# Choosing the PSUM bank of each product by three estimated clocks instead of a queue, in a fused adaLN, multi-query attention and gated-FFN kernel

## The chip, the cores and the metric

The kernel runs on one core of one Trainium2 chip. The metric is the device time of one execution in microseconds (us); a time given for a kernel is the median of several runs. The profile is that of one profiled execution. Engines are named as in its pages: PE is TensorE (PEld its weight loads), DVE is VectorE, ACT is ScalarE, POOL is GpSimd, SP is the queue that issues most DMAs. L601 is line 601 of the kernel before; in the kernel after, the lines up to the new functions' end and behind them lie up to eleven further on (L601 becomes L611, L511 becomes L521, L847 and L849 become L858 and L860).

## The reference

One transformer block on x of 2048 x 512, in float32, with a conditioning vector c of 512:

```python
mod = (silu(c) @ w_mod).reshape(1, 6, 1, 512)        # sa, ca, ga, sb, cb, gb
h = layernorm(x) * (1 + ca) + sa
q, k, v = h @ wq, h @ wk, h @ wv                     # 32 query heads of 16; one key and one value head
o = softmax(q @ k.T * 16 ** -0.5) @ v
x = x + ga * (o @ wo)
h = layernorm(x) * (1 + cb) + sb
x = x + gb * (((h @ w_gate) * (h @ w_up)) @ w_down)  # inner width 1792
```

## The kernel before

**The work and its stages.** Sequence rows are cut in eight sub-blocks of 256 (`sb`) and the 32 heads in four chunks, which gives 32 attention units `u`. For a unit TensorE makes, per key tile of 128, the scores `sc` (L657, L659) that ScalarE turns into exponentials `P` (L661), and from these the sums `pv` (L670: four fp32 products, eight records in the profile). The softmax needs the row maxima: for the next unit TensorE makes products `mx` (L601) that VectorE reduces to one column (`mpart`, L605). For unit 0, in the start, the maxima of later keys are made in another way: a `diff` product (a bank named `sc`, two matmuls at L601) is clipped by ScalarE (`rel`, L608), and a `both` product (a bank named `mx`) is added to it and reduced by VectorE (L610).

Everything else is "side work" in groups (class `Group`, L491): the query projection, the output projection `wo`, gate and up products (24 matmuls of 128 x 256 where a group runs whole), and down products (42 of 128 x 512). A group accumulates in one bank named `side` (all at L511), and is then emptied: a gate/up group by `g` on ScalarE (L847) and `gf` on VectorE (L849), a `wo` or down group by one residual add on VectorE (L750, L865). Between the attention's matmuls the side work fills in as half-array products; there are styles of a turn (L58 to L60), without side work, with few and with many. After the last unit's last `pv` comes the tail: all groups still left run whole, one behind the other: the last gate/up and down groups of sub-block 6, the last `wo` (L735), the last layer norm with its transposes to `mx` banks (L805, emptied by two `hf` on ScalarE each, L813), and all 14 gate/up and 2 down groups of sub-block 7 (`cover`, `run`, L1327 to L1355).

**The order.** It is written out while the program is built: the code calls the products in the order in which each engine gets them, and no scheduler reorders them. The hardware's part is only the semaphores: the first matmul into a bank waits until the bank's last reader is done.

**The banks.** PSUM has eight banks of 128 x 512 floats, and `pool` (L77) is a queue of their names. `ps_hold` (L80) takes the bank at the queue's head, `ps_give` (L87) puts it at the end; `ps_mx` (L91) does both at once, so for `mx` and `sc` the queue turns with each product. `side` groups and `pv` hold their bank until they are emptied (L519, L677), one or two groups and one `pv` at a time. So a bank comes round again some five to seven allocations later, whoever read it.

**The staging slots.** In the start, weights are loaded into slots of 512 floats in `kwb` (`hfs`, L225; `SLOTS`, L35; `stage`, L931), where GpSimd squares them (L944, L946). The sums of squares `ssqs` (L226) lie in the same tile; the first one covers slots 4 to 7.5, so with slots 6 and 7 in `SLOTS` it shares their place. `kng` (L227), which only the `diff` products read, lies in the first half of slot 12.

Of the kernel before, what the change touches and what calls it, by code (L numbers as in the profile page):

```python
# [13 lines left out]
F32 = mybir.dt.float32  # L14
# [8 lines left out]
BT = S // NB  # L23
# [8 lines left out]
SQ_GAP = 2.6  # L32
LAG = 2
ROW_LAG = 4
SLOTS = (0, 1, 2, 3, 6, 7)  # L35
SUM_GAP = 4.0
SUM_LAG = 3
SPLIT_GAP = 2.5
# [1 line left out]
LATE_Q = 3  # L40
NORM_AT = (5, 12, 15, 19)
NBANK = 8
QPRE = 24
Q_LAG = 8
TR_WAIT = 11
# [18 lines left out]
def adaln_mqa_glu_kernel(ctx: ExitStack, tc: tile.TileContext, x_in, wq_in, wk_in, wv_in, wo_in,  # L64
# [9 lines left out]
    psum = ctx.enter_context(tc.tile_pool(name="psum", bufs=1, space=bass.MemoryType.PSUM))  # L74
    ctx.enter_context(tc.manual_schedule())

    pool = deque((f"bank{i}", 1) for i in range(NBANK))  # L77
    held = {}

    def ps_hold(name="side", shape=(128, 512)):  # L80

        tag, bufs = pool.popleft()
        t = psum.tile(list(shape), F32, name=name, tag=tag, bufs=bufs)
        held[id(t)] = (t, tag, bufs)
        return t

    def ps_give(t):  # L87
        _, tag, bufs = held.pop(id(t))
        pool.append((tag, bufs))

    def ps_mx(name="mx", shape=(128, 512)):  # L91
        t = ps_hold(name, shape)
        ps_give(t)
        return t

    def ps_sc():
        return ps_mx("sc")

    def ps_misc(shape=(128, 512)):
        return ps_mx("misc", shape)  # L100
# [45 lines left out]
    for i in range(3):  # L146
        t = consts.tile([128, 2, 2, ST], F16, name=f"sst{i}")
# [15 lines left out]
    nc.gpsimd.memset(selk, 0.0)  # L163
    nc.gpsimd.memset(selq, 0.0)
    pwarm = ps_hold("misc")

    def keep_warm(n):
# [17 lines left out]
    sil = consts.tile([128, KC], F32, name="sil")  # L185
    csb = consts.tile([128, KC], F32, name="csb")
    pc = ps_mx()
    nc.tensor.transpose(pc[:, 0:KC], c4, ident[0:KC, 0:KC])
    nc.scalar.activation(csb, pc[:, 0:KC], AF.Copy)
# [34 lines left out]
    kwb = big.tile([128, 2 * FT * D], F16, name="kwb", tag="wd")  # L224
    hfs = kwb[:, 0:2 * NHF * BT].bitcast(F32).rearrange("p (n t) -> p n t", n=NHF)  # L225
    ssqs = [kwb[:, 2 * n * BT:2 * n * BT + 2 * F].bitcast(F32) for n in (KC, 2 * KC)]  # L226
    kng = kwb[:, 2 * NHF * BT:2 * NHF * BT + BT]  # L227

    def hf(b, k):
# [33 lines left out]
    def ln_tr(b, ks=range(KC)):  # L263
        for k in ks:
            p = ps_sc()
            for t in range(4):
                nc.tensor.transpose(p[:, t * 128:(t + 1) * 128],
                                    xts[2 * b + t // 2][t % 2][:, k * 128:(k + 1) * 128], ident)
            bias, scale = (hsb[:, k, 0:1], hsb[:, k, 1:2]) if b else (modT[0][:, k, 0:1], modT[0][:, k, 32:33])
            nc.scalar.activation(hf(b, k), p, AF.Identity, bias=bias, scale=scale)  # L270
# [3 lines left out]
    def partial(key, ws, b):  # L274
        p = ps_hold("part")
        w = BT // len(ws)
        for j in range(KC):
            for c, wc in enumerate(ws):
                nc.tensor.matmul(p[32 * j:32 * j + 32, c * w:(c + 1) * w], wc[:, j], hf(b, j)[:, 0:w],
                                 start=True, stop=True)  # L280
        parts[key] = work.tile([128, BT], F32, name="part", tag="ev", bufs=3)
        nc.scalar.activation(parts[key], p, AF.Copy)
        ps_give(p)
# [11 lines left out]
    def q_evac(u, p):  # L295
        split_rows(sst[u][:, :, p, :], pks[u, p], qsc, sck[:, 3:4], 0.0)
        ps_give(pks[u, p])
# [122 lines left out]
    def wq_sum():  # L420
        p = ps_sc()
        nc.tensor.matmul(p[:, 0:4], ones, wst["acc"], start=True, stop=True)
        t = work.tile([128, 2], F32, name="wqt", bufs=1)
        nc.vector.tensor_reduce(t[:, 0:1], p[:, 0:4], axis=AX.X, op=OP.add)
        nc.gpsimd.tensor_tensor(t[:, 1:2], t[:, 0:1], phalf[:, 0:1], op=OP.pow)
        nc.gpsimd.tensor_scalar(inv[:, 1:2], t[:, 1:2], 1.001 * 2.0 ** -15, 2.0 ** -45, op0=OP.mult, op1=OP.max)
# [132 lines left out]
    def load_q(u):  # L559
        sb, ch = divmod(u, NC)  # L560
        d = qd[sb // 2, ch].rearrange("(h e) l n -> e h l n", e=16)
        s = sst[u % 3].rearrange("p c q n -> p (c q) n")
        n0 = (sb % 2) * ST
        for a in range(2):
            for r, hl in ((0, 0), (1, 0), (2, 1)):
                nc.sync.dma_start(s[64 * a + 16 * r:64 * a + 16 * r + 16, :, :], d[:, a::2, hl, n0:n0 + ST])
# [26 lines left out]
    def max_mm(u, a, op):  # L593
        kind, p, t, kc = op
        s = sst[u % 3]
        m = ps_sc() if kind == "diff" else ps_mx()
        keys = [kst[:, kc * 512:(kc + 1) * 512]]
        if kind == "diff":
            keys = [kng, kst[:, (kc + 1) * 512:(kc + 2) * 512]]
        for i, w in enumerate(keys):  # L600
            nc.tensor.matmul(m, s[64 * a:64 * a + 48, t // 2, p, t % 2 * 128:(t % 2 + 1) * 128], w[64 * a:64 * a + 48, :],  # L601
                             start=(i == 0), stop=(i == len(keys) - 1))
        part = mparts[u][:, a, 4 * (t // 2) + 2 * p + t % 2, kc:kc + 1]
        if kind == "one":
            nc.vector.tensor_reduce(part, m, axis=AX.X, op=OP.max)  # L605
        elif kind == "diff":
            r = rel[a] = work.tile([128, 512], F32, name="rel", tag="x1", bufs=6)
            relus.append(lambda: nc.scalar.activation(r, m, AF.Relu))  # L608
        else:
            nc.vector.tensor_tensor_reduce(out=rel[a], in0=m, in1=rel[a], scale=1.0, scalar=LOW, op0=OP.add,  # L610
                                           op1=OP.max, accum_out=part)  # L611
# [53 lines left out]
    def pv(u, kt):  # L665
        if kt == 0:
            pvb[u] = ps_hold("pv")
        for j in range(4):
            p, a = divmod(j, 2)
            nc.tensor.matmul(pvb[u][32 * j:32 * j + 32, :], vst[:, kt, :], ptl[u, kt, p, a],  # L670
                             start=(kt == 0), stop=(kt == KT - 1))
# [221 lines left out]
    def late_weights():  # L893
# [35 lines left out]
        taken = [0]  # L929

        def stage(n):  # L931
            if "d" in W:
                t = work.tile([128, D], F32, name="wsl", tag="xl", bufs=3)
            else:
                t = hfs[:, SLOTS[taken[0] % len(SLOTS)], :]
                taken[0] += 1
            nc.sync.dma_start(t[:, :sl[n][3]], sl[n][2])
            st[n] = t
# [24 lines left out]
        def norms(order):  # L963
            ns = [n for m in order for n in range(len(sl)) if sl[n][0] == m]
            out = []
            waiting = deque()
            for j in range(len(ns) + LAG):
                q = j - LAG

                def f(j=j, q=q):  # L970
                    if j < len(ns):
                        stage(ns[j])
                    if q >= 0:
                        square(ns[q])
                out.append((SQ_GAP, nothing, f))
                if waiting and j >= waiting[0][0]:
                    out.append((0,) + sums(*waiting.popleft()[1:]))
                if q >= 0 and (q == len(ns) - 1 or sl[ns[q]][0] != sl[ns[q + 1]][0]):
                    waiting.extend((j + SUM_LAG, sl[ns[q]][0], n) for n in range(4))
            out.append((SUM_GAP, nothing, nothing))  # L980
            return out + [(2,) + sums(*w[1:]) for w in waiting]
# [146 lines left out]
    def max_half(a):  # L1128
# [10 lines left out]
        u, i, last, ops = flat[n]  # L1139
        if 0 < u < NU - 1 and i == QPRE:  # L1140
            load_q(u + 1)
# [76 lines left out]
    def attend(u, kt):  # L1218
# [10 lines left out]
        def end_turn(kt):  # L1229
            for g in ended:  # L1230
                g.finish()
            ended.clear()
            for f in ends:
                f()
            ends.clear()
            v = u * KT + kt - 1
            if v >= 0:
                pv(*divmod(v, KT))
                if v % KT == KT - 1:
                    ends.append(lambda: pv_out(u - 1))  # L1240
            if not late_max() and turns and all(q.ended() for q in qs):
                _, f, post = turns.popleft()
                f()
                posts.append(post)
            hooks(u, 2 * kt + 1)
# [66 lines left out]
    u = NU - 1  # L1312

    pv(u, KT - 1)
    pv_out(u)
    sync["before"] = sync["exp"]
# [60 lines left out]
```

## Time and profile before

| | |
|---|---|
| median of 3 runs | 1665.09 us (1664.6 to 1665.9) |
| span of the profiled execution, first to last instruction | 1663.8 us |
| median less that span | 1.3 us |
| PE busy | 1643.3 us (99%) |
| DVE busy | 1402.3 us (84%) |
| ACT busy | 1234.8 us (74%) |
| POOL busy | 523.5 us (31%) |
| granted TensorE clock, mean | 0.998 |

The profiled execution has no time of its own beside the span. A row of a group gives line, engine, operation, tile written and read, and count; behind it the busy time, the mean of one in ns, the idle time of the engine just before, and what ended that. A row of the windows gives a stretch (from:to, us) and each engine's busy time in it, with the granted clock behind. A row in order of time gives start, duration and what; in square brackets stands the idle time before it and what released it. Matmuls overlap each other, so a busy PE may still issue late. The span falls in four parts: the start to about 80 us, attention with little side work to about 320 us, attention with side work to about 1552 us, and the tail.

### The profile page before, as it was taken

Reading aid. Unit: us, or ns where it says so; the run is one execution under the profiler, and the core shown is the slowest. Engines: PE = TensorE matmul, PEld = TensorE weight load, DVE = VectorE, ACT = ScalarE, POOL = GpSimd, SP = SyncE. Lnnn points to the kernel's source line nnn. Section 1 sums busy time; section 2 is a strip of 40 time slices with the busy share of each in tenths; the row PEclk is TensorE's granted clock in tenths of the full one; section 3 lists DMA queues with packets and bytes.
Section 4 is the critical chain, followed back from the end, with each engine's and each line's share of the span. In section 5 each row is a group of like instructions: output and inputs, shape, how many; then the busy total and the mean of one; then the engine's idle time right before and its main releaser. Section 6 shows DMA issues by size and latency. Waiting matters only on the chain.

```text
span 1663.8 us, 39821 instructions
## 1 busy us (share of the span) xinstructions
PE 1643.3 (99%) x15677; PEld 747.1 (45%) x15677; DVE 1402.3 (84%) x2434; ACT 1234.8 (74%) x2389; POOL 523.5 (31%) x833
## 2 busy tenths in 40 slices
PE   8899999999999999999999999999999999999999
PEld 4333333355533554335543355434545345454776
DVE  7999999998998999899998999999998999980211
ACT  5688888888777877777877787777878777877300
POOL 4857537864841111301112011300113001210322
PEclk9999999999999999999999999999999999999999
DMA  6313313342210001000000000000000000000100
GB/s 237 108 59 100 95 43 120 96 129 80 77 51 24 18 12 32 19 32 20 20 26 23 25 13 24 26 25 26 20 29 15 26 22 20 26 14 21 33 13 14
DMA packets 66024, 75.39 MB, mean 45 GB/s; under 512 B 17702, under 2 KB 46634, under 8 KB 65836
## 3 DMA queue, kind: packets, MB, share of 16 engines
q1 hardware_dynamic: 63724, 72.26, 13.7%
q8 instruction: 123, 2.02, 0.5%
q10 hardware_dynamic: 2112, 0.59, 0.1%
q14 instruction: 65, 0.53, 0.1%
HBM read 55.51 MB, written 17.04 MB: 44 GB/s over the span
## 4 chain that ended last, share of the span: by engine, by line
PE 93%; ACT 2%; DVE 2%; DMA 1%; issue 1%; POOL 0%; SPq 0%; ACTq 0%; DVEq 0%
PE side L511 41%; PE pv L670 30%; PE mx L601 8%; PE sc L659 8%; PE sc L657 3%; ACT P L661 2%; DVE mpart L605 1%; DMA xbig<-in_A_x_dram 1%; PE mx L805 1%; PE mxt L629 0%; ACT hf L813 0%; PE sc L601 0%; DVE bs L248 0%; DMA kwb<-in_B_w_down_dram 0%; DMA wkv<-in_A_wv_dram 0%
## 5 line engine op out<-in xcount | busy, mean ns | idle before, releaser
L605 DVE TENSOR_REDUCE mpart<-mx 128x1 f32<-128x512 f32 x2016 | 1274.1, 684 | 104.0 <-PE mx L601 95.7
L661 ACT ACTIVATE P<-sc 128x512 f32<-128x512 f32 x2048 | 1094.8, 598 | 274.2 <-PE sc L659 226.9
L601 PE MATMUL mx<-kst,sst 48*128 48x512 f16 x2032 | 631.5, 377 | 3.8 <-ACT P L661 1.7
L659 PE MATMUL sc<-sst,kst 50*128 50x512 f16 x1792 | 597.5, 379 | 0.6 <-ACT P L661 0.3
L670 PE MATMUL pv<-P,vst 128*32 128x512 f32 x4096 | 545.3, 605 | 0.7
L511 PE MATMUL side<-h2T,wg 64*128 64x256 f16 (+1 forms) x2396 | 540.8, 271 | 0.1
L511 PE MATMUL side<-h2T,wu 64*128 64x256 f16 (+1 forms) x2396 | 538.7, 270 | 0.0
L511 PEld LDWEIGHTS <-wg 64*128 64x128 f16 (+1 forms) x2396 | 226.0, 94 | 230.5 <-ACT P L661 194.0
L511 PE MATMUL side<-wd,glu 64*128 64x512 f16 (+1 forms) x1172 | 272.8, 378 | 0.2 <-ACT P L661 0.2
L850 POOL TENSOR_SCALAR glu<-gf 128x256 f16<-128x256 f32 x112 | 45.8, 409 | 671.3 <-DVE gf L849 583.9
L511 PEld LDWEIGHTS <-wu 64*128 64x128 f16 (+1 forms) x2396 | 226.4, 94 | 43.0 <-issue 7.8
L601 PEld LDWEIGHTS <-sst 48*128 48x128 f16 x2064 | 189.9, 94 | 34.2 <-issue 17.4
L659 PEld LDWEIGHTS <-kst 50*128 50x128 f16 x1792 | 162.9, 94 | 63.0 <-issue 50.3
L511 PEld LDWEIGHTS <-glu 64*128 64x128 f16 (+1 forms) x1172 | 98.5, 94 | 192.4 <-ACT P L661 85.9
L670 PEld LDWEIGHTS pv<-P,vst 128*32 128x32 f32 x4096 | 80.7, 108 | 160.9 <-issue 150.1
L849 DVE TENSOR_TENSOR gf<-side,g 128x256 f32<-128x256 f32 x112 | 46.7, 418 | 79.8 <-ACT g L847 77.7
L657 PE MATMUL sc<-sst,kst 50*128 50x256 f16 x512 | 96.9, 268 | 0.1
L511 PE MATMUL side<-h,wq 64*128 64x512 f16 (+1 forms) x372 | 95.0, 376 | 0.4 <-ACT P L661 0.4
L847 ACT ACTIVATE g<-side 128x256 f32<-128x256 f32 x112 | 42.3, 379 | 65.6 <-PE side L511 65.3
L511 PE MATMUL side<-wo,och 64*128 64x512 f16 (+1 forms) x360 | 86.3, 377 | 0.0
L851 POOL TENSOR_TENSOR glu<-gf,glu 128x256 f16<-128x256 f32 x112 | 75.3, 673 | 9.3
L706 POOL TENSOR_TENSOR oc<-oc,rr 128x256 f32<-128x256 f32 x31 | 22.7, 731 | 146.6 <-DMA rr<-ri 100.4
(233 smaller groups left out, 865.4 us busy)
## 6 DMA issues: line engine op xcount, KB each, us to landing
pd<-ev SPq DMA_DIRECT2D x32, 256.0 KB
kwb<-in_B_w_gate_dram SPq DMA_DIRECT2D x32, 224.0 KB
kwb<-in_B_w_up_dram SPq DMA_DIRECT2D x32, 224.0 KB
sst<-qd SPq DMA_DIRECT2D x180, 32.0 KB
qd<-q SPq DMA_DIRECT2D x16, 256.0 KB
oc<-pd SPq DMA_DIRECT2D x64, 64.0 KB
rr<-ri SPq DMA_DIRECT2D x64, 64.0 KB
x<-in_A_x_dram SPq DMA_DIRECT2D x14, 256.0 KB
```

What stands on the lines that cost most here:

```text
L511: return nc.tensor.matmul(self.p[:, c * w:(c + 1) * w], left[rows], right[rows], start=start and c == 0, stop=stop and c == len(terms) - 1)
L601: nc.tensor.matmul(m, s[64 * a:64 * a + 48, t // 2, p, t % 2 * 128:(t % 2 + 1) * 128], w[64 * a:64 * a + 48, :], start=(i == 0), stop=(i = ...
L605: nc.vector.tensor_reduce(part, m, axis=AX.X, op=OP.max)
L657: nc.tensor.matmul(t[:, c * ST:(c + 1) * ST], keys, s[64 * a:64 * a + 50, c, p, :], start=True, stop=True)
L659: nc.tensor.matmul(t.rearrange("k (c n) -> k c n", c=2), keys, s[64 * a:64 * a + 50, :, p, :], start=True, stop=True)
L661: ex = nc.scalar.activation(ptl[u, kt, p, a], t, AF.Exp)
L670: nc.tensor.matmul(pvb[u][32 * j:32 * j + 32, :], vst[:, kt, :], ptl[u, kt, p, a], start=(kt == 0), stop=(kt == KT - 1))
L706: eng.tensor_tensor(o, o, st["r"], op=OP.mult)
L847: nc.scalar.activation(g, p[:, 0:ST], AF.Copy, scale=2.0 ** -45)
L849: nc.vector.tensor_tensor(gf, p[:, ST:2 * ST], g, op=OP.mult)
L850: nc.gpsimd.tensor_scalar(glu()[:, 0, f, :], gf, 1.0, 0.0, op0=OP.mult, op1=OP.add)
L851: nc.gpsimd.tensor_tensor(glu()[:, 1, f, :], gf, glu()[:, 0, f, :], op=OP.subtract)
```

## The change

Each bank now carries a time at which its reader should be done. Three clocks `est` (for PE, ACT and DVE) are kept while the program is built, in the units of `EST`: each `ps_mx` product moves PE's clock by 0.22 and its reader's to the later of that clock and PE's plus 0.45, plus 0.49 (ACT) or 0.6 (DVE); each `pv` call moves PE's by 1.15. A product takes the bank with the least time (`min(banks)`: of equal times the lowest bank number), and PE's clock moves up to that time. A bank given back without an engine's name (by groups, `pv`, `part`, `pk` and the like) is marked with the largest of the three clocks, and no clock moves. Beside it two staging slots change from 6 and 7 to 12 and 13.

```diff
-SLOTS = (0, 1, 2, 3, 6, 7)
+SLOTS = (0, 1, 2, 3, 12, 13)
+EST = {"pe": 0.22, "lag": 0.45, "act": 0.49, "dve": 0.6, "pv": 1.15}
...
-    pool = deque((f"bank{i}", 1) for i in range(NBANK))
+    banks = [[0.0, i] for i in range(NBANK)]
+    est = {"pe": 0.0, "act": 0.0, "dve": 0.0}
     held = {}
 
     def ps_hold(name="side", shape=(128, 512)):
 
-        tag, bufs = pool.popleft()
-        t = psum.tile(list(shape), F32, name=name, tag=tag, bufs=bufs)
-        held[id(t)] = (t, tag, bufs)
+        b = min(banks)
+        banks.remove(b)
+        est["pe"] = max(est["pe"], b[0])
+        t = psum.tile(list(shape), F32, name=name, tag=f"bank{b[1]}", bufs=1)
+        held[id(t)] = (t, b[1])
         return t
 
-    def ps_give(t):
-        _, tag, bufs = held.pop(id(t))
-        pool.append((tag, bufs))
+    def ps_give(t, engine=None):
+        _, n = held.pop(id(t))
+        if engine is None:
+            free = max(est.values())
+        else:
+            est["pe"] += EST["pe"]
+            free = est[engine] = max(est[engine], est["pe"] + EST["lag"]) + EST[engine]
+        banks.append([free, n])
 
-    def ps_mx(name="mx", shape=(128, 512)):
+    def ps_mx(name="mx", shape=(128, 512), engine="dve"):
         t = ps_hold(name, shape)
-        ps_give(t)
+        ps_give(t, engine)
         return t
 
     def ps_sc():
-        return ps_mx("sc")
+        return ps_mx("sc", engine="act")
...
+    stg = kwb.bitcast(F32).rearrange("p (n t) -> p n t", t=BT)
...
     def pv(u, kt):
         if kt == 0:
             pvb[u] = ps_hold("pv")
+        est["pe"] += EST["pv"]
...
-                t = hfs[:, SLOTS[taken[0] % len(SLOTS)], :]
+                t = stg[:, SLOTS[taken[0] % len(SLOTS)], :]
```

The instructions of each engine keep their order; what differs is the bank of a tile and so the semaphore that its first matmul waits for. Two places on PE show it. In the rows, `sc_776` and the like are tiles with their numbers (equal in both kernels), and in brackets stand the engines whose semaphore is waited for (`Activation_49` ACT, `DVE_49` DVE, `PE_49` PE itself).

In the start, in the steps of `diff` (`sc`) and `both` (`mx`) products of unit 0, PE has before:

```order
L601 MATMUL sc_776<-kwb_181,sst0_128 128x512
L601 LDWEIGHTS sst0_128
L601 MATMUL sc_776<-kst_132,sst0_128 128x512
L601 LDWEIGHTS sst0_128
L601 MATMUL mx_786<-kst_132,sst0_128 128x512
```

and eight rows further on:

```order
L601 MATMUL mx_793<-kst_132,sst0_128 128x512 [waits DVE_49]
L601 LDWEIGHTS sst0_128
L601 MATMUL sc_796<-kwb_181,sst0_128 128x512 [waits DVE_49]
L601 LDWEIGHTS sst0_128
L601 MATMUL sc_796<-kst_132,sst0_128 128x512
```

The same places after:

```order
L611 MATMUL sc_776<-kwb_181,sst0_128 128x512 [waits Activation_49]
L611 LDWEIGHTS sst0_128
L611 MATMUL sc_776<-kst_132,sst0_128 128x512
L611 LDWEIGHTS sst0_128
L611 MATMUL mx_786<-kst_132,sst0_128 128x512
```

```order
L611 MATMUL mx_793<-kst_132,sst0_128 128x512
L611 LDWEIGHTS sst0_128
L611 MATMUL sc_796<-kwb_181,sst0_128 128x512 [waits Activation_49]
L611 LDWEIGHTS sst0_128
L611 MATMUL sc_796<-kst_132,sst0_128 128x512
```

A `diff` product now waits for ACT, where it waited for nothing or for DVE: `sc_776` has the bank of `sc_769`, `sc_796` that of `sc_776`, and so on; the `both` product `mx_793` waits for nothing any more.

In the tail, where the gate/up group that began before the last `wo` ends (`side_26291`) and the next one begins (`side_26394`), PE has before:

```order
L511 LDWEIGHTS wu_4056
L511 MATMUL side_26291<-h2T_4878,wu_4056 128x256
L511 LDWEIGHTS wg_4055
L511 MATMUL side_26394<-h2T_4878,wg_4055 128x256
L511 LDWEIGHTS wu_4056
```

and after:

```order
L521 LDWEIGHTS wu_4056
L521 MATMUL side_26291<-h2T_4878,wu_4056 128x256
L521 LDWEIGHTS wg_4055
L521 MATMUL side_26394<-h2T_4878,wg_4055 128x256 [waits DVE_49]
L521 LDWEIGHTS wu_4056
```

The first matmul of `side_26394` waited for nothing, since its bank had long been read; now it has the bank of `side_26291` and waits for DVE's read of that. The same difference stands in the gate/up groups of the last sub-block, before:

```order
L511 MATMUL side_26690<-h2T_4878,wu_4056 128x256
L511 LDWEIGHTS wg_4055 [waits PE_49]
L511 MATMUL side_26721<-h2T_4878,wg_4055 128x256 [waits Activation_49]
L511 LDWEIGHTS wu_4056
L511 MATMUL side_26721<-h2T_4878,wu_4056 128x256
```

and after:

```order
L521 MATMUL side_26690<-h2T_4878,wu_4056 128x256
L521 LDWEIGHTS wg_4055
L521 MATMUL side_26721<-h2T_4878,wg_4055 128x256 [waits DVE_49]
L521 LDWEIGHTS wu_4056
L521 MATMUL side_26721<-h2T_4878,wu_4056 128x256
```

Before, `side_26721` had the bank of the second transpose tile, seven allocations back, which ACT reads; after, that of `side_26690`, the group directly before it.

## Prediction

> **What bounds the kernel now.** I read the page's busy shares first, then the chain that ended last, then the windows of two stretches, and then the instructions in order of time at the places where a bank is waited for.
>
> ```profile
> span 1663.8 us, 39821 instructions
> PE 1643.3 (99%) x15677; PEld 747.1 (45%) x15677; DVE 1402.3 (84%) x2434; ACT 1234.8 (74%) x2389; POOL 523.5 (31%) x833
> PE 93%; ACT 2%; DVE 2%; DMA 1%; issue 1%; POOL 0%; SPq 0%; ACTq 0%; DVEq 0%
> ...
> core 0: us, PE busy (x) PEld busy (x) DVE busy (x) ACT busy (x) POOL busy (x), PEclk, DMA share, GB/s
> 320.00:1500.00 1180.00, 1176.83 (x11971) 539.52 (x11965) 1079.19 (x1820) 933.51 (x1806) 282.79 (x465) 1.00 0.11 32
> 1552.00:1660.00 108.00, 107.84 (x796) 77.58 (x793) 21.53 (x44) 13.62 (x32) 31.51 (x66) 1.00 0.06 21
> ```
>
> TensorE bounds it: 93% of the chain. But a busy PE hides small waits, since a matmul of 0.38 us is issued every 0.22 us. So for the middle stretch I count turns (one turn is one `pv` step of 8 recorded matmuls), and set them against a turn in which nothing waits:
>
> ```profile
> 320.00:1500.00 1180.00, 429.94 (x3232) 63.44 (x3224) 17.11 (x25) 1.00 0.11 32
> ...
> 800.70 1.06 PE L670 MATMUL pv<-P,vst 128*32 128x512 f32 x8
> ...
> 803.55 1.07 PE L670 MATMUL pv<-P,vst 128*32 128x512 f32 x8
> ...
> 806.47 1.07 PE L670 MATMUL pv<-P,vst 128*32 128x512 f32 x8
> ```
>
> The first row is the middle stretch for tile `pv` alone: 3232/8 = 404 turns in 1180 us, 2.92 us each. The three starts below it give one turn of 2.85 and one of 2.92 us. 404 x 2.85 = 1151, so all waits and all extra work in the middle come to 1180 - 1151 = 29 us. That is everything a better choice of banks could win there. Transposes of the row maxima and of h2 lie in it too (some 70 matmuls, about 0.1 us each): 29 - 7 = 22 us is the ceiling.
>
> The last 110 us are another regime: PE is busy for 107.84 of 108 us with VectorE at 21.53 and ScalarE at 13.62. Each group fills a bank of its own, and the small chain that empties it runs under the next groups. One boundary between two gate/up groups:
>
> ```profile
> 1615.24 0.27 PE L511 MATMUL side<-h2T,wu 128*128 128x256 f16 x1
> 1615.35 0.27 PE L511 MATMUL side<-h2T,wg 128*128 128x256 f16 x1
> ...
> 1615.55 0.38 ACT L847 ACTIVATE g<-side 128x256 f32<-128x256 f32 x1 [2.24 <-PE side L511]
> ...
> 1616.03 0.42 DVE L849 TENSOR_TENSOR gf<-side,g 128x256 f32<-128x256 f32 x1 [2.19 <-ACT g L847]
> ```
>
> The old group's last matmul starts at 1615.24, the next group's first at 1615.35, 0.11 later. The old bank is empty only when the DVE row ends, 1616.03 + 0.42 = 1616.45. The queue hides this, because the bank comes up again only some seven groups later.
>
> **The change part by part.** It adds and removes no instruction and moves none on any engine; what it changes is which bank each product writes, and so what its first matmul waits for.
>
> *The tail.* A bank handed back without an engine's name gets the largest of the three clocks. Only `ps_mx` and `pv` advance the clocks, and neither is called again after the last `pv` (two calls of `ps_hold` for the h2 transposes aside, which also hand back without a name). So every bank is soon marked with one and the same time, and `min` of equal times takes the lowest number: the bank just handed back. The built program agrees: from `side_26350` on, 24 groups in a row take the bank of the group directly before, as does the second transpose tile. TensorE runs in program order, so it now waits out the whole emptying 25 times; what is queued behind is all the rest of PE's work, and the groups' outputs wait for PE.
>
> A gate/up boundary costs, from the rows above: from the last matmul's start to the bank's release 1616.45 - 1615.24 = 1.21, plus a hop to PE, minus the 0.11 it takes today. The hops in these rows are 0.04 (PE to ACT) and 0.10 (ACT to DVE); I take 0.05: 1.15 us. Nineteen of the 24 follow a gate/up group: 19 x 1.15 = 21.9 us. Four follow a group that VectorE empties alone:
>
> ```profile
> L511 PE MATMUL side<-wd,glu 128*128 128x512 f16 x172 | 37.6, 379 | 0.0
> ...
> 1596.00 0.75 DVE L865 SCALAR_TENSOR_TENSOR x<-side,sca,x 128x512 f32<-128x512 f32 x1 [8.16 <-PE side L511]
> ...
> 1605.07 0.75 DVE L865 SCALAR_TENSOR_TENSOR x<-side,sca,x 128x512 f32<-128x512 f32 x1 [8.31 <-PE side L511]
> ```
>
> 42 matmuls in 9.07 us are 0.22 each; the wait is 0.38 + 0.04 + 0.75 + 0.05 - 0.22 = 1.0; four make 4.0 us. One boundary is far dearer, because ScalarE stands behind the last layer norm there:
>
> ```profile
> 1572.53 0.75 DVE L750 SCALAR_TENSOR_TENSOR x1p<-side,sca,x1p 128x512 f32<-128x512 f32 x1 [0.89 <-PE side L511]
> ...
> 1576.86 0.81 ACT L771 ACTIVATE n<-x1p,nb,ry 128x512 f32<-128x512 f32 x1 [1.78 <-POOL nb L764]
> 1577.58 0.64 ACT L847 ACTIVATE g<-side 128x256 f32<-128x256 f32 x2
> ...
> 1578.04 0.76 DVE L849 TENSOR_TENSOR gf<-side,g 128x256 f32<-128x256 f32 x2 [3.82 <-ACT g L847]
> ...
> 1579.08 1.48 ACT L813 ACTIVATE hf<-mx,hsc 128x256 f32<-128x256 f32 x3
> ```
>
> The group finished just after the attention output (`side_26291`) ends its matmuls at about 1572.7, four matmuls after the `wo` group of the first row, but its `g` comes after the second `n`. Today PE goes on to other banks. Afterwards PE stands from there until the first `gf` ends, about 1578.04 + 0.42 = 1578.46, and both ends move with the stall before it: 1578.46 + 0.05 - 1572.76 = 5.75 us. The second transpose tile waits for two `hf` (half of four, about 1.0 us) behind a transpose of 0.3: 1.3 us. The tail's sum: 21.9 + 4.0 + 5.8 + 1.3 = 33.0 us. Nothing covers it: PE had 0.16 us idle in those 108 us, and every stall shifts all that follows.
>
> *The clock.* A stall of 5.8 us is longer than any of today's after the first loads. What a shorter one did:
>
> ```profile
> 55.63 0.58 PE L601 MATMUL sc<-kst,sst 48*128 48x512 f16 x1 [2.06 <-DVE kst L304]
> ...
> 36.00:50.00 14.00, 12.34 (x82) 6.41 (x80) 13.53 (x24) 12.83 (x25) 10.06 (x18) 1.00 0.59 226
> ...
> 55.00:62.00 7.00, 6.37 (x30) 2.93 (x31) 7.00 (x18) 4.89 (x9) 6.67 (x8) 0.52 0.01 2
> ```
>
> After 2.06 us without a matmul the granted clock was 0.52 in the next 7 us; with PE busy 12.34 of 14 it stayed at 1.00. So I count one such spell after the 5.8 us: about 7 us at half clock with PE working some 0.7 of it (2.6 of each 3.8 us) loses 7 x 0.7 / 2 = 2.4; I take 2 (0 to 4). The shorter stalls of 1.15 us I count at full clock, by the row of 36 to 50. [...]
>
> *The start.* In the first unit's `diff`/`both` steps each `diff` bank is emptied by ScalarE and each `both` by VectorE. The built program gives a `diff` the bank of the `diff` of its own half one step earlier; the queue gave it one from two steps earlier.
>
> ```profile
> L601 PE MATMUL sc<-kwb,sst x16: 373/631/631, 53.2 to 64.3; 48*128 48x512 f16 x16
> ...
> L608 ACT ACTIVATE rel<-sc 128x512 f32<-128x512 f32 x16 | 8.5, 605 | 3.9 <-PE mx L601 2.8 <-PE sc L601 0.9
> L610 DVE CUSTOM_DVE_ANT_0 rel<-mx,rel 128x512 f32<-128x512 f32 x16 | 9.9, 689 | 0.0
> ```
>
> At half clock (0.63 us a matmul, issued 0.43 apart) a step then takes 0.43 + 0.63 + 0.04 + 0.60 + 0.05 = 1.75 us, against two DVE passes of about 0.65 (0.69 each, overlapping a little) = 1.3: some 0.45 lost in each of about five steps, 2.3 us; at full clock the loop is about 1.3 and nothing is lost. In the first attention turns two `sc` take a bank whose exponential has just begun, because the ScalarE clock knows none of the start's other work: +1 (0 to 3). Given back may be up to 1.6 us, since PE waits for GpSimd later anyway:
>
> ```profile
> PE mx L956 <- POOL kwb L946: 1.6, 1, 1.6
> ```
>
> I take 3 us for the start, -1 to 8.
>
> *The middle.* The tiles keep their order, and VectorE its load (1079 of 1180 us). In the built program about two thirds of the allocations there (2191 of 3394) take over the bank of the very same tile as before, and where the tile differs, its reader ended earlier in this trace about as often (568 times) as later (635). So the clocks mostly rename the banks that the queue chose. I take +1; from -12 (half the ceiling won) to +4 (an estimate: a fifth of it lost).
>
> *The staging slots.* Two of six staging places move off the sums of squares. That lifts waits of transfers behind GpSimd, which runs at 31% and for which PE waits once (the 1.6 us): 0, at best -1.6.
>
> Sum: 33.0 + 2 + 3 + 1 = 39. The profiled span is 1663.8, the median 1665.09, 1.3 of it outside the span; 1665.1 + 39 = 1704.
>
> **The rivals.** *The middle wins what it can (the other side).* The estimated clocks would steer every product off a late bank between 320 and 1500 us: at most 22 us. If the tail's emptying were at the same time hidden as today, the time is 1665 - 22 = 1643. It decides only if the gain is above the tail's 33, which the ceiling excludes unless the tail's waits are missing; the rule that `min` takes the lowest of equal times is in the code, and PE has no second stream. For it: 93% of the chain on PE, with small gaps in many turns. Chance 0.02. *Half of the ceiling is won and the tail is paid:* 1704 - 12 = 1692; chance 0.10. *The start costs more*, the half clock lasting through its steps: 8 instead of 3 and 4 in the middle, 1712; chance 0.10. *The tail stays at half clock:*
>
> ```profile
> 1579.48 80.38 PE side L511 x572
> ```
>
> 80 us of matmuls after the long stall, with a gap of 1.15 in each 3.8 us; at half clock throughout they would take 80 more: 1784, and 1744 if half of the time. Against it: 12.34 of 14 us busy kept 1.00, and the tail would be busy to some 0.7. [...] Chance 0.06. *The change does nothing* (banks ready anyway): 1665; 0.01.
>
> **How the numbers follow.** The forecast, 1704, has the rest, 0.71. The range goes from 1690 (half the middle's ceiling won, no loss of clock) to 1720 (start 8, middle 4, clock 4, hops of 0.1 for the tail's: 1665 + 33 + 1 + 16, and 5 for a second spell of half clock); it leaves out the half-clock tail and the rare gains. A measurement of this kernel tells 0.2% (3.3 us) from no change; faster 0.02, same 0.01, slower 0.97.
>
> **What would show it.** Right: PE's waits for the DVE lines of `gf` and the residual adds appear, some 25 of them and above 25 us in all (none today); consecutive `g` in the tail stand 3.8 us apart instead of 2.62; PE's chain share falls and ACT's and DVE's rise; one spell of low clock near the end; `pv` turns in the middle at 2.92 as before. Wrong: `g` still 2.62 apart, or turns at 2.85 throughout.

## The result and the profile after

The kernel after takes 1711.87 us (median of 4 runs, 1711.62 to 1712.05) where the kernel before, on the same chip, takes 1665.49 (1664.6 to 1667.12): a ratio of 1.0277, 95% interval 1.0263 to 1.029. It is slower by 46.4 us. The profiled execution of after took 1711.95 us, 1.75 of it outside its span of 1710.2.

The same three places of the page of after (span, busy times, shares of the chain that ended last):

```profile
span 1710.2 us, 39799 instructions
PE 1657.0 (97%) x15677; PEld 749.4 (44%) x15677; DVE 1402.5 (82%) x2434; ACT 1236.2 (72%) x2389; POOL 523.1 (31%) x833
PE 92%; ACT 4%; DVE 2%; issue 1%; DMA 1%; POOL 0%; ACTq 0%; DVEq 0%; SPq 0%
```

The work is the same to the instruction count of each engine; DVE, ACT and POOL are busy for as long as before. PE's busy time rose by 13.7 us with the same 15677 matmuls. About 4 us of that is overlap lost in the tail, where the last matmul before a wait now runs alone (33.4 us lost there, 29.2 of it idle, as shown below); the rest is mainly matmuls at half clock (30.7 us of it in after, 6.8 in before). PE's share of the chain fell in favour of ACT, while DVE's stayed at 2%. The rest of the 46 us is idle time. What PE's matmuls waited for (total us, times, longest) tells where:

```profile
PE side L521 <- DVE gf L860: 24.8, 20, 5.6
PE pk L297 <- ACT vst L330: 2.8, 1, 2.8
PE sc L611 <- ACT rel L618: 2.1, 8, 0.7
PE side L521 <- DVE x L876: 1.7, 2, 0.8
PE mx L967 <- POOL kwb L957: 1.6, 1, 1.6
...
PE mx L816 <- ACT hf L824: 1.1, 1, 1.1
...
PE side L521 <- DVE x1p L876: 0.8, 1, 0.8
PE side L521 <- DVE x1p L761: 0.8, 1, 0.8
```

Rows one, four and the last three are the tail: 25 waits, 29.2 us. None of them was there before. Rows two and three are the start: a bank that ACT's `vst` had not yet read, and the `diff` loop. The row of GpSimd (POOL) stands at 1.6 us as before.

I set the start of each matmul in after against that of the same matmul in before. The lag in three stretches:

| stretch | lag at its end | grown by |
|---|---|---|
| start, to the side work's full speed (after about 100 us) | 11.86 us | 11.9 |
| middle, to the last groups before the last `wo` | 10.72 us | -1.1 |
| tail, to the last matmul | 46.35 us | 35.6 |

**The tail.** ACT's `g` in the last sub-block of after, in order of time (start, duration, idle before and its releaser):

```profile
1644.35 0.38 ACT L858 ACTIVATE g<-side 128x256 f32<-128x256 f32 x1 [3.40 <-PE side L521]
1648.13 0.38 ACT L858 ACTIVATE g<-side 128x256 f32<-128x256 f32 x1 [3.40 <-PE side L521]
1651.91 0.38 ACT L858 ACTIVATE g<-side 128x256 f32<-128x256 f32 x1 [3.40 <-PE side L521]
```

They stand 3.78 us apart. One boundary between groups, and the long one behind the last `wo`, from all engines' rows in order of time:

```profile
1636.47 0.27 PE L521 MATMUL side<-h2T,wu 128*128 128x256 f16 x1
...
1636.78 0.38 ACT L858 ACTIVATE g<-side 128x256 f32<-128x256 f32 x1 [23.53 <-PE side L521]
1637.27 0.42 DVE L860 TENSOR_TENSOR gf<-side,g 128x256 f32<-128x256 f32 x1 [3.36 <-ACT g L858]
1637.75 0.27 PE L521 MATMUL side<-h2T,wg 128*128 128x256 f16 x1 [1.00 <-DVE gf L860]
```

```profile
1584.37 0.27 PE L521 MATMUL side<-h2T,wu 128*128 128x256 f16 x1
...
1588.58 0.81 ACT L782 ACTIVATE n<-x1p,nb,ry 128x512 f32<-128x512 f32 x1 [2.78 <-POOL nb L775]
1589.30 0.36 ACT L858 ACTIVATE g<-side 128x256 f32<-128x256 f32 x1
1589.76 0.42 DVE L860 TENSOR_TENSOR gf<-side,g 128x256 f32<-128x256 f32 x1 [3.82 <-ACT g L858]
1590.24 0.37 PE L521 MATMUL side<-h2T,wg 128*128 128x256 f16 x1 [5.59 <-DVE gf L860]
```

The last `wu` matmul starts at 1636.47 and the next group's first at 1637.75, 1.28 later instead of 0.11: 1.17 lost, of which the profile shows only 1.00 as idle, since the last matmul still runs for 0.27. Most of the 19 ordinary boundaries cost 1.16 to 1.17. At the long one it is 1590.24 - 1584.37 - 0.11 = 5.76 us, and the row of `n` shows why: ACT's `g` stands behind it.

**The clock.** Four stretches of after (from:to, PE busy and so on, with the granted clock third from the end), in two answers, first the start, then the tail:

```profile
45.00:49.00 4.00, 3.72 (x12) 2.58 (x13) 1.92 (x4) 1.58 (x5) 1.28 (x2) 0.57 0.58 239
...
59.00:79.50 20.50, 18.36 (x73) 4.00 (x76) 15.26 (x43) 9.06 (x17) 17.48 (x23) 0.50 0.00 1
```

```profile
1588.00:1595.00 7.00, 4.76 (x23) 3.39 (x23) 0.42 (x1) 1.08 (x2) 1.45 (x4) 0.52 0.00 0
1595.00:1700.00 105.00, 82.19 (x584) 56.81 (x583) 12.56 (x26) 9.34 (x23) 20.40 (x38) 1.00 0.02 8
```

After the long stall there is one spell of half clock of 6.8 us; then, with a pause in every 3.78 us, the clock stays at 1.00 to the end. In the start the half clock lasts 20.5 us, where before it was 6.8.

**The start.** PE at the place where `pk` waits, first before, then after:

```profile
41.08 0.60 PE L601 MATMUL mx<-kst,sst 48*128 48x512 f16 x4
43.06 1.13 PE L287 MATMUL pk<-part,selk 128*128 128x512 f32 x2 [1.38 <-ACT part L282]
```

```profile
41.60 0.86 PE L611 MATMUL mx<-kst,sst 48*128 48x512 f16 x4
45.28 2.00 PE L297 MATMUL pk<-part,selk 128*128 128x512 f32 x2 [2.82 <-ACT vst L330]
```

And ACT's `rel` in the `diff` loop, before and after:

```profile
56.25 0.60 ACT L608 ACTIVATE rel<-sc 128x512 f32<-128x512 f32 x1 [2.80 <-PE mx L601]
...
60.97 1.09 ACT L608 ACTIVATE rel<-sc 128x512 f32<-128x512 f32 x2 [0.19 <-PE sc L601]
62.25 3.54 ACT L608 ACTIVATE rel<-sc 128x512 f32<-128x512 f32 x7 [0.19 <-PE sc L601]
```

```profile
59.63 0.60 ACT L618 ACTIVATE rel<-sc 128x512 f32<-128x512 f32 x1 [2.65 <-PE mx L611]
61.32 1.08 ACT L618 ACTIVATE rel<-sc 128x512 f32<-128x512 f32 x2 [1.10 <-PE sc L611]
...
64.77 1.09 ACT L618 ACTIVATE rel<-sc 128x512 f32<-128x512 f32 x2 [0.61 <-PE sc L611]
66.46 1.08 ACT L618 ACTIVATE rel<-sc 128x512 f32<-128x512 f32 x2 [0.61 <-PE sc L611]
...
73.23 0.60 ACT L618 ACTIVATE rel<-sc 128x512 f32<-128x512 f32 x1 [0.61 <-PE sc L611]
```

The wait at `pk` is 2.82 us instead of 1.38. There the lag goes from 0.52 to 2.22 us, and to 3.38 by the first `rel` (59.63 - 56.25), with a 3.4 us spell of half clock in between. The loop itself takes 73.23 - 59.63 = 13.60 us from the first `rel` to the last, where before it took 62.25 + 3.54 - 0.60 - 56.25 = 8.94: another 4.7. A step is 1.69 us (66.46 - 64.77) against 1.28 (62.25 - 60.97). The pace before is that of VectorE's two passes: it had no pause from its first pass to its last, 57.88 to 67.23 us; after, it is idle in front of every step (0.1 to 0.4 us) and needs 61.48 to 74.00, 3.2 us more. The rest of the 4.7 is ACT's: in before's last steps it ran ahead of VectorE, 0.96 us a step. The half clock that outlasts the loop adds 2.2, and the first attention turns 1.6: 3.4 + 4.7 + 2.2 + 1.6 = 11.9.

**The middle.** The stretch of the middle in after, moved by its lag, for tile `pv` alone:

```profile
332.00:1511.00 1179.00, 430.10 (x3232) 63.42 (x3224) 17.11 (x25) 1.00 0.11 32
```

The same 3232 records, so 404 turns, in 1179 us instead of 1180: 2.92 us a turn, as before. The -1.1 of the lag isn't the change's: in e4, e2 and e8 (below), whose banks in this stretch are chosen as in the kernel before, the lag falls by 1.0, 1.7 and 1.1 us in the same place, between 360 and 400 us. It belongs to the profiled execution of before.

### The profile page after: what moved, and what is told of

Its sections match the earlier page's. It is cut to its first block, busy times and chain, and to the rows that moved or that the text cites. A ratio compares the mean times of both kernels' runs of the same rounds, so it can differ in the third digit from the quotient of the medians.

```text
span 1710.2 us, 39799 instructions
## 1 busy us (share of the span) xinstructions
PE 1657.0 (97%) x15677; PEld 749.4 (44%) x15677; DVE 1402.5 (82%) x2434; ACT 1236.2 (72%) x2389; POOL 523.1 (31%) x833
## 4 chain that ended last, share of the span: by engine, by line
PE 92%; ACT 4%; DVE 2%; issue 1%; DMA 1%; POOL 0%; ACTq 0%; DVEq 0%; SPq 0%
PE side L521 40%; PE pv L681 29%; PE mx L611 8%; PE sc L669 8%; PE sc L667 3%; ACT P L671 2%; DVE mpart L615 1%; DMA xbig<-in_A_x_dram 1%; PE mx L816 1%; PE sc L611 1%; DVE gf L860 1%; ACT g L858 0%; PE pk L297 0%; PE mxt L639 0%; ACT hf L824 0%
```

## The experiments

The theory after the result: the tail's waits for the bank just handed back make some 35 us; the start makes the rest, in three places (the wait of `pk`, the `diff` loop with its half clock, the first attention turns); the clocks do next to nothing in the middle. The rivals: the middle carries part of the loss, or hides a gain that the start eats; and in the start, either the bank wait or the clock is what counts. In the table, each kernel stands against the kernel before on the same chip.

| kernel | median us (range, runs) | before there | ratio, 95% interval |
|---|---|---|---|
| e1_tail_oldest | 1676.47 (1675.03 to 1678.04, 4) | 1665.31 | 1.0065, 1.0051 to 1.0079 |
| e2_tail_one_bank | 1697.09 (1696.52 to 1698.65, 4) | 1665.31 | 1.019, 1.0176 to 1.0204 |
| e3_middle_only | 1667.48 (1665.67 to 1671.18, 11) | 1665.31 | 1.0016, 1.0006 to 1.0025 |
| e4_slots_only | 1665.56 (1664.03 to 1666.32, 11) | 1665.31 | 0.9998, 0.9989 to 1.0006 |
| e5_clocks_from_diff | 1673.28 (1670.94 to 1674.12, 4) | 1665.98 | 1.0042, 1.0027 to 1.0057 |
| e6_queue_in_diff | 1671.57 (1670.63 to 1674.74, 4) | 1665.98 | 1.004, 1.0026 to 1.0053 |
| e7_from_unit1 | 1665.62 (1664.31 to 1666.76, 11) | 1665.98 | 0.9999, 0.999 to 1.0008 |
| e8_tail_two_banks | 1672.15 (1668.68 to 1672.5, 5) | 1665.57 | 1.0039, 1.0025 to 1.0054 |
| e9_full_clocks | 1664.27 (1662.12 to 1665.75, 11) | 1665.98 | 0.999, 0.9981 to 0.9999 |
| e10_diff_kept_warm | 1676.99 (1676.72 to 1677.44, 4) | 1665.57 | 1.0069, 1.0054 to 1.0084 |
| e11_diff_gap_filled | 1671.83 (1670.06 to 1673.88, 5) | 1665.59 | 1.0035, 1.0022 to 1.0047 |
| e12_full_clocks_gap_filled | 1664.31 (1661.85 to 1665.73, 11) | 1665.59 | 0.999, 0.9981 to 0.9999 |

### The tail with the queue's choice (e1_tail_oldest)

The kernel after, but from the last `pv` on a product takes the bank given back longest ago:

```diff
+    oldest = [False]
...
-        b = min(banks)
+        b = banks[0] if oldest[0] else min(banks)
...
+    oldest[0] = True
```

> The kernel after, but from the last pv on a tile takes the bank that was given back longest ago. Theory (the tail's tie sends every group into the bank just given back): the 25 waits and the spell of low clock behind the long one go, 33.4 + 2.2 = 35.6 us; 1711.9 - 35.6 = 1676, and g in the tail stands 2.62 us apart again. Rival (the tail is slow for the low clock alone, which the start's or the middle's order brings about): only some 2 us go, 1709.

Measured: 1676.47, as the theory had it, 35.2 us less of a gap to before than the kernel after has (46.4 - 11.2). PE's waits in it begin so:

```profile
PE pk L298 <- ACT vst L331: 2.8, 1, 2.8
PE mx L198 <- DMA c<-in_c_dram: 2.2, 1, 2.2
PE sc L612 <- ACT rel L619: 2.1, 8, 0.7
```

The row of `gf` is gone, and the two rows of the start stand as in after. The tail is worth 35 us, and the start's loss doesn't depend on it.

### The tail's choice alone, in the kernel before (e2_tail_one_bank)

The kernel before; in the tail it takes the bank with the lowest number among those given back since the tail began:

```diff
+        if stale[0] is None or pool[0][0] in stale[0]:
+            tag, bufs = pool.popleft()
+        else:
+            tag, bufs = min(pool)
+            pool.remove((tag, bufs))
+        if stale[0]:
+            stale[0].discard(tag)
...
+    stale[0] = {tag for tag, _ in pool}
```

> The kernel before, queue and all, but in the tail a tile takes the lowest-numbered bank of those given back since the last pv. Theory: the tail's cost stands alone and needs nothing of the clocks: 1665.5 + 33 to 36 = 1699 to 1702. Rival (the cost arises together with the shifted start or middle): clearly less than 33.

Measured: 1697.09, 31.8 us over before, a little under what was expected. Its first bank wait of the tail:

```profile
PE side L518 <- DVE gf L856: 20.8, 19, 2.7
```

19 waits with a longest of 2.7, where after has 20 with a longest of 5.6: here `side_26394` gets the bank of the last `wo` group, which VectorE's add frees after a wait of 0.4 us, and only the group behind it waits for ACT's late `g`. That is why less was lost than expected. Without any clock in the program the choice of the bank just handed back makes the loss: 18 ordinary waits of (20.8 - 2.7)/18 = 1.01 idle us, as in after.

### Two banks in the tail (e8_tail_two_banks)

The kernel before; the tail's groups share two banks:

```diff
-        tag, bufs = pool.popleft()
+        tag, bufs = next(x for x in pool if not two or (x[0] in two) == (name == "side"))
+        pool.remove((tag, bufs))
...
+    two += [tag for tag, _ in pool][:2]
```

> The kernel before, but in the tail all groups share two banks (the older one first); the transposes use others. Theory (a group's 2.62 us of matmuls cover the 1.2 us in which the bank before it is emptied): the gate/up and down boundaries of the last sub-block cost nothing; only around the last layer norm, where two groups wait for a g behind n, 4.7 us and perhaps a spell of low clock: 1670 to 1672. Rival (any reuse within two groups costs as the reuse of one): 1690 or more.

Measured: 1672.15, just above what was expected. The waits of its tail in the profiled execution, the shortest of the five (1668.68):

```profile
PE side L513 <- DVE gf L851: 2.4, 1, 2.4
...
PE side L513 <- DVE x1p L752: 1.2, 2, 0.8
```

Three waits are left, all around the last `wo` and the layer norm, and not one at an ordinary boundary. Two banks are enough there: one group's matmuls (2.62 us) cover the 1.2 us in which the other bank is emptied. The 3.5 us between this execution and the median are not in these waits; the mean granted clock was 0.998 in it and 0.995 or 0.996 in the other four, so half clock is the likely reason, but there is no trace of those.

### The clocks in the middle alone (e3_middle_only, e7_from_unit1)

e3: the kernel after, with the longest-free bank in the start and in the tail. e7: the clocks begin only with the second unit's turns.

```diff
+    oldest = [True]
...
-        b = min(banks)
+        b = banks[0] if oldest[0] else min(banks)
...
+    oldest[0] = False
...
+    oldest[0] = True
```

> The clocks choose the bank only between the end of the start and the last pv; before and after it the oldest bank is taken; staging slots as after. Theory (the clocks mostly rename the queue's banks): 1665.5 - 1 = 1664 to 1665, within 0.2% of before. Rival (the clocks win in the middle and the start's shift hid it): 1655 or less. Rival (they lose there): 1669 or more.

Measured: 1667.48, above what was expected; the lag in its profile shows a step of 1.6 us in the first attention turns (between 75 and 100 us). Behind them it drifts up to 2.4 and back to 0.1: the profiled execution, 1665.67, is the fastest of the eleven, and the median's 2.2 us are in no trace. So e7 was set to begin behind these turns, at the second unit:

```diff
-    oldest[0] = False
...
+            oldest[0] = False
```

> As the kernel with the clocks in the middle alone, but the clocks start one attention unit later (some 40 us), so that the first turns take the oldest bank. Theory (its 2 us over before come from the first turns, where sc took the bank of an exponential just begun): 1665 to 1666, within 0.1% of before. Rival (they come from the long middle): 1667.5 as it was.

Measured: 1665.62, ratio 0.9999. The step is gone with the first turns (there is none in its profile), and the clocks from there to the tail are worth 0 within the interval of 0.1%. Neither the ceiling of 22 us nor half of it is won.

### The staging slots alone (e4_slots_only)

```diff
-SLOTS = (0, 1, 2, 3, 6, 7)
+SLOTS = (0, 1, 2, 3, 12, 13)
...
-                t = hfs[:, SLOTS[taken[0] % len(SLOTS)], :]
+                t = stg[:, SLOTS[taken[0] % len(SLOTS)], :]
```

> The kernel before with the two staging slots alone moved from 6 and 7 to 12 and 13. Theory: 1665.5, within 1.6 us, since GpSimd's waits there lie beside PE's work. Rival (the slots bring part of the start's 12 us, by transfers that wait for the products which read kng): 1668 or more.

Measured: 0.9998, no difference.

### The start in two parts (e5_clocks_from_diff, e6_queue_in_diff)

Both have the queue's choice in the tail. e5 takes the clocks from the `diff` steps on, e6 takes them ahead of the `diff` steps and behind them:

```diff
     for n in range(LEAD):
+        oldest[0] = n < 14
```

(e5; steps 14 and up hold the `diff` products)

```diff
     for n in range(LEAD):
+        oldest[0] = n >= 14
...
+    oldest[0] = False
```

(e6, which begins with `oldest = [False]`)

> Oldest bank up to step 14 of the start and in the tail, the clocks from the diff/both steps on; against the kernel with the clocks in the middle alone (1667.5). Theory (the diff banks, read by ScalarE one step before, stretch the loop by themselves): 8 steps x 0.4 = 3.3 more, and up to 3 for a longer half clock: 1671 to 1674; diff starts 1.7 us apart. Rival (the loop is only slow since the early stall at the pk product drops the clock): 1667 to 1669, diff starts 1.3 us apart.

> The counterpart: clocks up to step 14 of the start, oldest bank in the diff/both steps and in the tail, clocks in between. Theory: the stall at the pk product (3.0 us) stays, with one or two spells of half clock behind it: 1667.5 + 3 to 6 = 1670.5 to 1673.5; diff starts 1.3 us apart. Rival (the two parts need each other): within 1 us of 1667.5.

Measured: 1673.28 and 1671.57, both as the theory had it. Taken against e3 in gaps to the kernel before (2.2 us), the `diff` steps cost 7.3 - 2.2 = 5.1 us and the steps ahead of them 5.6 - 2.2 = 3.4; both together, e1, cost 11.2 - 2.2 = 9.0, about their sum. In e5 the half clock lasted 20.5 us again, with the `rel` pairs 1.69 apart, though `pk` waited no longer than in before: it belongs to the `diff` loop. (That execution, the slowest of the four, has another 3.4 us of half clock from 85.7 us on.) So the start's parts are 3.4 to 4 for the wait of `pk`, 5 to 5.6 for the loop and the half clock behind it, and 2.5 for the first turns (e3 less e7, 2.2 + 0.4). They are rough, since the intervals reach 1.5 to 2.5 us to either side, and those of e3 and e7 overlap a little. The lag in after gives 3.4, 6.9 and 1.6; the 1.6 stands in the profiles of e1, e3, e6 and e11 as well.

### Is it the clock or the bank wait in the loop? (e10_diff_kept_warm, e11_diff_gap_filled)

At full clock the prediction's step of the loop is 1.29 us, as fast as DVE; at half clock 1.75. e10 is e5 with one spare 128x512 matmul per step into a bank of its own, to keep PE at work. That bank (`pwarm`, used for a warm-up before) is given back only behind the loop, so all else in the start has seven banks instead of eight:

```diff
-    ps_give(pwarm)
...
+            if 14 < n < 25:
+                nc.tensor.matmul(pwarm, kst[:, 0:128], kst[:, 0:512], start=True, stop=True)
...
+    ps_give(pwarm)
```

> The kernel with the clocks from the diff steps on (1673.3), with one spare 128x512 matmul more per step of the start from step 15 to 24 into a bank of its own, which no one reads. Theory (the loop stays slow since PE, waiting in it, is never busy enough for the full clock to come back: 20.5 us at half): the half clock ends some 7 us after it began, diff starts come down from 1.7 to about 1.3 us, 1669 to 1671 although work was added. Rival (the bank wait alone makes the loop, whatever the clock): 1673 or more, diff starts 1.7 apart.

Measured: 1676.99, slower than e5. The `rel` rows and the stretch of the loop in e10:

```profile
64.12 1.08 ACT L618 ACTIVATE rel<-sc 128x512 f32<-128x512 f32 x2 [0.92 <-PE sc L611]
66.23 1.09 ACT L618 ACTIVATE rel<-sc 128x512 f32<-128x512 f32 x2 [1.03 <-PE sc L611]
```

```profile
59.00:79.00 20.00, 19.86 (x66) 4.54 (x65) 13.27 (x39) 8.29 (x16) 16.59 (x22) 0.50 0.00 1
```

PE is busy for 19.86 of 20 us, and the clock is still at 0.50; the steps take 2.1 us, since the spare matmuls take time of their own at half clock (0.61 us each). The theory that more work brings the clock back fell. Not all that e10 is slower than e5 is the loop's: in the profiles 2.0 us of it stand ahead of the loop already, where e10 has the seven banks and a spell of half clock of 3.4 us (from 45.3 us on) that e5 doesn't have. e11 therefore fills the wait *ahead* of the loop, 2.06 us in which PE waits for the copy of the keys:

```diff
+            if (u, a, p, t) == (0, 0, 0, 0):
+                for _ in range(9):
+                    nc.tensor.matmul(m, s[0:48, 0, 0, 0:128], kng[0:48, :], start=True, stop=True)
```

> The kernel e5_clocks_from_diff with nine spare 48x512 matmuls into the bank of the first `diff` product ahead of its own two, so that PE works through the 2.06 us in which it stands for the copy of the keys. Theory (the stand starts the low clock, and the low clock is what turns the bank wait into a loss): no spell of half clock from 55 to 75 us; a step then takes 0.22 + 0.38 + 0.04 + 0.60 + 0.05 = 1.29 us, so the `rel` pairs stand about 1.3 us apart instead of 1.69, and the time falls from 1673.3 by some 3 to 5 us, to 1668 to 1670. Rival one (the bank wait alone makes the loop, whatever the clock): pairs still 1.6 to 1.7 us apart at full clock, time 1672 to 1674. Rival two (the low clock is begun by something else): half clock still there in the loop, pairs 1.69, time 1672 to 1674.

Measured: 1671.83, between what the theory and the rivals gave and nearer to the rivals; the interval of its ratio overlaps e5's. But its loop shows both states in one execution:

```profile
57.56 0.60 ACT L622 ACTIVATE rel<-sc 128x512 f32<-128x512 f32 x1 [2.58 <-PE mx L615]
58.84 1.09 ACT L622 ACTIVATE rel<-sc 128x512 f32<-128x512 f32 x2 [0.68 <-PE sc L615]
60.17 1.25 ACT L622 ACTIVATE rel<-sc 128x512 f32<-128x512 f32 x2 [0.25 <-PE sc L615]
61.86 1.25 ACT L622 ACTIVATE rel<-sc 128x512 f32<-128x512 f32 x2 [0.45 <-PE sc L615]
63.56 1.25 ACT L622 ACTIVATE rel<-sc 128x512 f32<-128x512 f32 x2 [0.44 <-PE sc L615]
```

```profile
56.00:60.00 4.00, 2.77 (x18) 0.95 (x18) 4.00 (x7) 1.68 (x3) 3.83 (x5) 1.00 0.00 0
60.00:74.00 14.00, 13.75 (x56) 2.73 (x54) 11.26 (x37) 7.77 (x13) 13.33 (x17) 0.51 0.00 1
```

With the clock at 1.00 the first steps stand 1.28 and 1.33 us apart, and VectorE has no pause in its first four passes (59.41 to 61.24 us): the bank wait costs the loop nothing there. From 60.3 us on the clock is at half, and the steps are 1.69 and 1.70. And the kernel before, with the queue's banks, is at half clock from 55.3 to 62.1 us and keeps its steps at 1.22 to 1.34. So it takes both, the bank of the step before and the half clock. That the wait of 2.06 us is what starts the half clock is shown wrong: with it filled, the clock falls all the same, 2.7 us into a loop in which PE is busy for 2.77 of 4 us. Why it falls there, and why e10's added work didn't hold it, stays open.

### Clocks that know all the work (e9_full_clocks, e12_full_clocks_gap_filled)

e9 is e7 with the clocks charged for what they left out, and with durations from the profile:

```diff
-EST = {"pe": 0.22, "lag": 0.45, "act": 0.49, "dve": 0.6, "pv": 1.15}
+EST = {"pe": 0.2135, "lag": 0.45, "act": 0.55, "dve": 0.635, "pv": 1.13}
...
+    def charge(**us):
+        end = est["pe"] + EST["lag"]
+        for engine, t in us.items():
+            end = est[engine] = max(est[engine], end) + t
+            end += 0.1
+        read[0] = end
...
+            charge(**self.cost)
             self.evict(self.p)
-            ps_give(self.p)
+            ps_give(self.p, "read")
```

> As the one before, and the clocks also count the other work: emptying of groups, pv, row maxima and h2 are charged to their engines (0.2 to 1.0 us each), the steps are set to the trace's 0.55 (ACT), 0.635 (DVE), 0.2135 and 1.13 (PE). Theory (the queue's banks are near what can be had, ceiling 22 us): 1663 to 1666. Rival (the clocks failed in the middle only because they were incomplete): 1658 or less.

> The kernel e9_full_clocks with the same nine spare matmuls ahead of the first `diff` product. Its `diff` loop goes at VectorE's pace (1.28 us a step) in the half clock already. Theory: the 6.8 us of half clock go, the loop stays at 1.28, and only the two or three steps behind the loop and ahead of it that PE paces gain: 0 to 1.5 us, so 1662.8 to 1664.3. Rival (the spare matmuls only move the low clock to a later stretch where PE is the limit): 1665 to 1667.

Measured: 1664.27 and 1664.31, both with a ratio of 0.999 (0.9981 to 0.9999). They are the fastest versions here, and the gain of 1 to 2 us is under the 0.2% that I took as the bound. The spare matmuls of e12 gain nothing: a spell of half clock of the same 6.8 us begins at 56.1 us (at 55.3 in before and at 56.8 in e9).

## Why the prediction was right

It gave 1704 us, range 1690 to 1720; the time is 1711.87. By its own terms, with the lag's growth in the profile beside them:

| term | predicted | measured |
|---|---|---|
| tail, waits | 33.0 | 33.4 |
| of it 19 gate/up boundaries | 1.15 each | 1.16 to 1.17 each, a few 1.21 to 1.23 |
| of it four behind an add | 1.0 each | 1.006 each |
| of it the long one | 5.75 | 5.76 |
| of it the second transpose tile | 1.3 | 1.33 |
| tail, clock | 2 (0 to 4) | 2.2 |
| start | 3 (-1 to 8) | 11.9 |
| middle | 1 (-12 to 4) | -1.1 |
| slots | 0 | 0 (e4) |

**The tail was right, in mechanism and in size.** Every boundary could be worked out from the rows of before, since the chain that empties a bank was there, only hidden. e1 takes the loss away, e2 makes it without the clocks.

**The start was the step that failed:** "I take 3 us for the start, -1 to 8". The time is 7.9 us above the forecast: 8.9 more in the start, 2.1 less in the middle, 0.6 more in the tail with its clock, and 0.5 outside the span and by rounding. The start came out above its own range; the total stayed in the prediction's because its upper end keeps room for the middle, the clock, the hops and a second spell too, of which little was used. Three pieces of the start were wrong:

- There was no term for the steps ahead of the `diff` products. I had looked at the loop and at the first turns; `pk` there took over the bank that `vst` on ACT reads late, and waited 2.8 us instead of 1.4, with a spell of half clock behind it. In the start the clocks knew the readers of `ps_mx` products alone, and none of ACT's and DVE's other work. e6 against e3: 3.4 us.
- The loop's step was right (1.75 predicted at half clock, 1.69 measured; 1.3 at full clock, 1.28 in e11), but I counted about five such steps, which is what the 6.8 us of half clock in before hold. It lasted 20.5, through all eight steps and nearly 6 us beyond: 4.7 + 2.2 us instead of 2.3. The rival in which the half clock lasts through the loop, with 8 us for the start and 1712 for the whole, came nearest, by luck: it had the start still 3.9 too small and the middle 5.1 too large.
- The first attention turns cost 1.6 by the lag and 2.5 by e3 less e7, against 1. And nothing of GpSimd's 1.6 us was given back.

**The middle neither wins nor loses,** as the count of renamed banks had it: +1 was forecast, -1.1 measured (which kernels with the queue's banks show too), and e7's 0.9999 settles it, with the two rivals that let the middle win (1643 and 1692). The turn stayed at 2.92 us.

**The tail at half clock (1744 to 1784) did not come.** PE waited 25 times in the tail, 23 of them behind the long stall, and the clock was 1.00 for 105 us behind the one spell, with 1.0 us of idle time in each 3.78. In the `diff` loop, with shorter pauses (0.20 to 0.66 us a step), the clock stayed at 0.50 for 20.5 us. The row from which the prediction took the one spell, half clock behind 2.06 us without a matmul, is no rule: in e8's profile, with the mean clock at 0.998 as in before, it stayed at 1.00 behind a wait of 2.4 us in the tail.

## What to carry to other kernels

A queue of buffers has a merit that is easily lost: it hands out the one that was given back longest ago, and needs no estimate for that. A planner that picks by estimated times needs estimates for all readers, also the groups and the odd products, and a tie must go to the buffer freed longest ago, not to the lowest number. To price reuse of a buffer, read from the trace how long its emptying takes behind its last write and how long the work in between is: with one bank each boundary here paid 1.16 us, with two none, because 2.62 us of matmuls cover it.

## What the runs showed of the hardware

- In these traces half clock came in whole pieces of 3.41 us. Leaving out what the end of the program cuts off, after has spells of 3.41, 20.48 and 6.83 us, before one of 6.83, e11 of 3.41 and 13.65 (mean clock 0.995), e1 of 6.83 and 17.07 (0.993): 1, 6 and 2; 2; 1 and 4; 2 and 5 pieces. Not every spell is the change's: e4 (mean clock 0.996) has one of 3.41 at 126 us, where before (0.998) has none, though the two differ in the staging slots alone, and it cost 1.5 us. In before and after the clock stood at 0.50 within each spell and at 1.00 outside. A busy PE was not enough to end a spell: PE was busy for 18.36 of 20.5 us in the `diff` loop of after, and for 19.86 of 20 in e10's, at 0.50 throughout. What ends one was not found.
- A wait of 2.06 or 2.8 us ahead of a spell is not what it takes: in e11 the longest wait in the 15 us ahead of the spell of 13.65 us was 0.7 us.
- The price of a wait depended on the clock: the same bank reuse cost 0.4 us a step at half clock and, in the two steps that e11 has of it, nothing at full clock (1.69 and 1.28 us a step), as the prediction's sum had it: a matmul of 0.63 instead of 0.38 us lengthens the way from bank to reader to bank, and DVE's two passes, which hide it, stay as long as they were (0.69 us each).
